# Third token tile from the transposed copy of x, with its statistics stored in front of two broadcasts, and tiles 4 and 5 split in front of tile 3's features

## The chip, the cores and the metric

One core of a Trainium2 chip runs the whole computation as one launch. The metric is the device time of one execution, in microseconds (us). The runs of the kernel before took 638.29, 639.42 and 639.43 us; their median is 639.42 us. All arithmetic is float32; matrix products are made of three passes over operands that are split in a rounded high part and a low remainder.

## What is computed

For x of 2048 tokens by 640 features:

```
xn = layernorm(x)
q, k, v = split(xn @ wqkv)                      # 32 heads of 20
phi(u) = [softmax(u @ w_phi), softmax(-(u @ w_phi))]   # per head
kv = sum over tokens of phi(k)^T v ;  z = sum over tokens of phi(k)
s = (phi(q) kv / (phi(q) z + 1e-6)) @ wo
g = silu(gelu(xn @ w1 + b1) @ w2 + b2)
out = x + s * g
```

The change lies in the first tenth of the execution, where the first six token tiles are normalized, their keys and values are projected, and their key features are made.

## The kernel before

Tokens come in 16 tiles of 128. The matrix unit (TensorE, PE) multiplies token tiles by the folded key weight (`wk_s`, five chunks of 128 rows) and by the value weight (`wv_s`). For that, each tile's normalized x must stand transposed in SBUF (features on partitions, tokens along the row) and split in a high and a low part (`xp`, and `b12` for two chunks of an odd tile). There are two ways to get it:

- **By TensorE.** A tile is loaded as it stands (`x_in`), its mean and variance are taken on VectorE (DVE) (`norm_a`: two bn_stats, one bn_aggr, one add, and a power of -0.5 on GpSimd (POOL)), it is normalized (`norm_b` on DVE, `norm_act` on ScalarE (ACT)), and `transpose_x` turns it by five TensorE transposes into PSUM. `plain` then writes the high part (ACT, L272) and the low part (DVE, L274, reading PSUM). Before, tiles 0, 1 and 2 go this way.
- **From the transposed copy.** The transposed x is loaded from `xt_in` (`one_load` for a single tile, `load_xr` for a pair). Mean and rstd must then lie along the row: they are stored to a small DRAM buffer (`st_dram`) and read back with a partition broadcast as `bc`. POOL subtracts the mean (`one_sub` L370, `pair_sub` L331), DVE multiplies by rstd (`one_plain` L374, `pair_mul` L336), and `plain` splits as above, but now its DVE part reads two SBUF tensors. Before, tile 3 goes this way alone, and tiles 4 and on in pairs.

Per tile t the key path is: `project(t, wk_s)` (30 matmuls of 128x320 into one of three PSUM buffers "A"), `feat1` (DVE: maximum L409, subtraction L412, both reading PSUM, minimum L415; then POOL L416 makes the negated half), `feat2` (ACT exponential L425), `key_fin` (DVE sums L433 and reciprocal L465, then POOL scales, L438). `value(t)` is a projection with `wv_s` and an ACT copy (L454). `kv_pair` accumulates two tiles.

Each engine runs its own instructions in the order of the program, which in this part is mostly the order of the calls in the code; the order in front of the loop over tiles 2 to 5, and in that loop, is written out by hand. SP issues nearly all DMAs, in its own order, and each DMA also waits for the one eight before it. In the loop, tile 3's turn makes its features, then `pair_plain(2)` splits tiles 4 and 5; tile 4's turn holds `pair_sub(3)` and `pair_mul(3)` for tiles 6 and 7, and then `fold_pair(0)`: twelve folding matmuls into two PSUM buffers, then four DVE operations (L188) on them, of which the third is the last to read the first buffer. `value(5)` needs that buffer.

Of the kernel before, what the change touches and what calls it, by code (L numbers as in the profile page):

```python
# [46 lines left out]
def hedgehog_gated_mlp_kernel(ctx: ExitStack, tc: tile.TileContext, x, xt_in, wqk, bd, wv, wo, w1, b1, w2, b2, out_t):  # L47
# [36 lines left out]
    def row(shape, dt, name):  # L84
        return rows.tile(shape, dt, tag="R", name=name)
# [144 lines left out]
    def norm_a(t):  # L230
        sm = small.tile([P, 16], F32, tag="st", name="st")
        nrm[t] = sm, stats(t, sm, None, sm[:, 14:15])
# [6 lines left out]
    def norm_act(t):  # L239
        sm, xt = nrm.pop(t)  # L240
        nc.vector.tensor_scalar(sm[:, 15:16], sm[:, 12:13], -1.0, sm[:, 14:15], op0=OP.mult, op1=OP.mult)
        nc.scalar.activation(xt[:], xt[:], AF.Identity, bias=sm[:, 15:16], scale=sm[:, 14:15])
        xns[t] = xt
# [4 lines left out]
    def load_xr(q):  # L248
        h, p = divmod(q, SLOTS)
        xr = slab(F32, "xr", (P, KC, W2))[:]  # L250
        src = xt_in.rearrange("(k p) (h o q t) -> p k h o q t", p=P, h=NH, o=2, q=SLOTS)[:, :, h, :, p]
        nc.sync.dma_start(xr[:, :, :P], src[:, :, 0])
        nc.sync.dma_start(xr[:, :, P:], src[:, :, 1])
        xrs[q] = xr
# [13 lines left out]
    def plain(q, o, v, only=slice(0, 2), hi=True, lo=None):  # L268
        parts = [(xp[:, 0:5, :, at(q)], v)] if o == 0 else [(beside(q), v[:, 0:2]), (xp[:, 5:8, :, at(q)], v[:, 2:5])]
        parts = parts[only]  # L270
        for dst, src in parts if hi else ():
            nc.scalar.activation(dst[:, :, 0, :], src, AF.Copy)  # L272
        for dst, src in parts if lo is None else ():
            nc.vector.tensor_tensor(dst[:, :, 1, :], src, dst[:, :, 0, :].bitcast(F32), op=OP.subtract)  # L274
        for dst, src in parts if lo else ():
            nc.gpsimd.tensor_tensor(dst[:, :, 1, :], src, dst[:, :, 0, :].bitcast(F32), op=OP.subtract)
# [61 lines left out]
    def pair_plain(q):  # L338
        for o in range(2):
            plain(q, o, xrs[q][:, :, o * P:(o + 1) * P])  # L340

    def one_load(t):
        q = t // 2
        h, p = divmod(q, SLOTS)
        xr = slab(F32, "xr", (P, KC, W2))[:]
        src = xt_in.rearrange("(k p) (h o q t) -> p k h o q t", p=P, h=NH, o=2, q=SLOTS)[:, :, h, t % 2, p]
        nc.sync.dma_start(xr[:, :, :P], src)
        xrs[t, "one"] = xr[:, :, :P]

    def one_stats(t):  # L350
        sm = small.tile([P, 16], F32, tag="st", name="st")
        ps = sm[:, 14:16]
        xt, st = xts.pop(t), sm[:, :12]
        for i in range(2):
            nc.vector.bn_stats(st[:, 6 * i:6 * i + 6], xt[:, i * HALF:(i + 1) * HALF])
        yield
        nc.vector.bn_aggr(sm[:, 12:14], st.rearrange("p (a b) -> p a b", a=2))
        nc.vector.tensor_scalar(ps[:, 1:2], sm[:, 13:14], LN_EPS, None, op0=OP.add)
        nc.gpsimd.tensor_tensor(ps[:, 1:2], ps[:, 1:2], mhalf[:], op=OP.pow)
        nc.vector.tensor_copy(ps[:, 0:1], sm[:, 12:13])  # L360
        nc.sync.dma_start(st_dram[t // 2, t % 2], ps)
        bc = row([P, P, 2], F32, "bc")
        nc.sync.dma_start(bc[:].rearrange("p t s -> p (t s)"),
                          st_dram[t // 2, t % 2].rearrange("p s -> (p s)").partition_broadcast(P))
        pld[t, "one"] = bc
        yield

    def one_sub(t):
        bc, xr = pld[t, "one"], xrs[t, "one"]
        nc.gpsimd.tensor_tensor(xr, xr, bc[:, None, :, 0].to_broadcast([P, KC, P]), op=OP.subtract)  # L370

    def one_plain(t):
        bc, xr = pld.pop((t, "one")), xrs.pop((t, "one"))
        nc.vector.tensor_tensor(xr, xr, bc[:, None, :, 1].to_broadcast([P, KC, P]), op=OP.mult)  # L374
        plain(t // 2, t % 2, xr)

    def transpose_x(t):
        q, o = divmod(t, 2)
        xn = xns.pop(t)
        ps = bankA()  # L380
        flat = ps[:].rearrange("p a b -> p (a b)")
        for k in range(KC):
            nc.tensor.transpose(flat[:, k * P:(k + 1) * P], xn[:, k * P:(k + 1) * P], ident[:])  # L383
        plain(q, o, flat[:, :D].rearrange("p (k t) -> p k t", t=P))
# [3 lines left out]
    def project(t, ws, mid=None, at_k=3):  # L388
        q, o = divmod(t, 2)
        ps = bankA()  # L390
        n = 0
        for k in range(KC):
            if k == at_k and mid is not None:
                mid()
            for a, b in PASSES:
                for hf in range(2):
                    nc.tensor.matmul(ps[:, hf, :HALF], stat_x(q, o, k, a),  # L397
                                     ws[k][:, b, hf * HALF:(hf + 1) * HALF],
                                     start=n == 0, stop=n == 3 * KC - 1)
                n += 1  # L400
        return ps
# [4 lines left out]
    def feat1(ps, later=None):  # L406
        p4 = heads(ps)
        mx = small.tile([P, 2, 16], F32, tag="mx", name="mx")
        nc.vector.tensor_reduce(mx[:], p4, axis=AX.X, op=OP.max)  # L409
        e = slab(F32, "e")[:]  # L410
        e5 = e.rearrange("p a (h s d) -> p a h s d", s=2, d=DH)
        nc.vector.tensor_tensor(e5[:, :, :, 0, :], p4, mx[:, :, :, None].to_broadcast([P, 2, 16, DH]),  # L412
                                op=OP.subtract)
        nr = small.tile([P, 2, 16], F32, tag="nr", name="nr")
        last_feat[0] = nc.vector.tensor_reduce(nr[:], e5[:, :, :, 0, :], axis=AX.X, op=OP.min)  # L415
        rest = lambda: nc.gpsimd.tensor_tensor(e5[:, :, :, 1, :], nr[:, :, :, None].to_broadcast([P, 2, 16, DH]),  # L416
                                               e5[:, :, :, 0, :], op=OP.subtract)
        if later is None:
            rest()
        else:  # L420
            later.append(rest)
        return e.rearrange("p a b -> p (a b)")

    def feat2(ef):
        nc.scalar.activation(ef, ef, AF.Exp)  # L425
        return ef
# [24 lines left out]
    def value(t, mid=None):  # L451
        ps = project(t, wv_s, mid)
        v, v3 = value_row()
        nc.scalar.activation(v3[:, :, :DH].rearrange("p (a h) d -> p a h d", a=2), heads(ps), AF.Copy)  # L454
        return v
# [12 lines left out]
    def key_fin(ef):  # L468
        scale_heads(ef, key_sums(ef))
        return ef  # L470
# [12 lines left out]
    def kv_pair(t):  # L483
        for u in (t, t + 1):
            kv_acc(u, phis.pop(u), vs.pop(u))
# [47 lines left out]
    def x_in(t, eng=None):  # L533
        xts[t] = load_x(t, eng)
# [13 lines left out]
    wv_raw = [load_raw(wv[c * P:(c + 1) * P, :]) for c in range(KC)]  # L548
    for t in (3, 4, 5):
        x_in(t)  # L550
    x_in(6)
    x_in(7)
    nc.sync.dma_start(b1t[:], b1)
    nc.sync.dma_start(b2t[:], b2)
    wv_s = []

    def split_v(c):
        wv_s.append(split_w(wv_raw[c][:], "wv", "dve" if c == 3 else "pool"))
# [10 lines left out]
    norm_a(1)  # L569
    fold_w(wkT, range(4, KC), "wk", wk_s)  # L570
    norm_act(1)
    norm_a(2)
    st3 = one_stats(3)
    next(st3)
    split_v(0)
    one_load(3)
    kvp[0] = bankB("kv")
    pk = project(0, wk_s, lambda: transpose_x(1), 4)
    split_v(1)
    next(st3)  # L580
    load_xr(2)
    norm_act(2)
    split_v(2)
    es[0] = feat1(pk)
    split_v(3)
    pk = project(1, wk_s, lambda: transpose_x(2))
    split_v(4)
    feat2(es[0])
    es[1] = feat1(pk)
    one_sub(3)  # L590
    pair_stats(4)
    vs[0] = value(0)
    pair_stats(5)
    wqT = load_fold(0, (nc.sync,) * KC)
    x_in(8)
    x_in(9)
# [8 lines left out]
    for t in range(2, 6):  # L605
        pk = project(t, wk_s)
        if t % 2:
            kv_pair(t - 3)
        es[t] = feat1(pk)
        if t == 4:  # L610
            next(vf[0])
        if t == 2:
            pair_sub(2)
            pair_stats(6)
            pair_stats(7)
            pair_mul(2)
        if t == 3:
            pair_plain(2)
        if t > 3:
            pair_stats(t + 4)  # L620
        if t in (3, 4, 5):
            spill(t - 3)
        if t == 5:
            x_in(10)
        if t == 4:
            pair_sub(3)
            pair_mul(3)
        vs[t] = value(t)
        if t >= 4:
            fold_pair(t - 4)  # L630
        if t == 5:
            next(vf[0])
        feat2(es[t])
        if t == 4:
            pair_plain(3)
        phis[t] = key_fin(es.pop(t))
    def q_back(c):
        sl = slab(F32R, "wqb")
        wq_b.append(sl)
        nc.sync.dma_start(sl[:, :, :HALF].bitcast(F32), wq_dram[c])  # L640
# [979 lines left out]
```

## Time and profile before

| | us |
|---|---|
| median of the three timed runs | 639.42 |
| the profiled execution | 637.78 |
| its span, first to last instruction | 636.1 |
| PE busy in the span | 631.3 |
| PE busy from 20 to 80 us | 60.0 of 60 |
| DVE busy from 20 to 80 us | 49.57 of 60 |
| POOL busy from 20 to 80 us | 40.38 of 60 |

PE is busy throughout, so what it does not have to do is time saved, and each wait that it is given is time lost. In the rows of the trace, a row's first number is its start in us from the span's start, the second its length; then follow engine, line, operation, what it writes and reads, and, in square brackets, how long the engine had been idle and what ended that. SPq rows are DMA issues.

### The profile page before, as it was taken

To read this page: it belongs to the slowest core of one execution; us is meant where nothing else is said; L and a number is where in the kernel's file an instruction comes from. 1 tells how busy PE (TensorE), PEld (TensorE's weight loads), DVE (VectorE), ACT (ScalarE), POOL (GpSimd) and SP (SyncE) were. 2 spreads that over 40 slices of the span, in tenths; PEclk is the share of its full clock that TensorE was granted. 3 is DMA by queue.
4 is the path that set the end of the run, shared out by engine and by line. 5 is a ranking of instruction groups with operands and counts; after the bars stand their busy time and mean duration, and the time that the engine had idled before them with its cause. 6 is when DMAs were issued, how large, how long until landed. Compare 5 with 4: busy or idle time off the path is not lost.

```text
span 636.1 us, 11441 instructions
## 1 busy us (share of the span) xinstructions
PE 631.3 (99%) x4324; PEld 550.3 (87%) x4324; DVE 511.1 (80%) x790; ACT 259.7 (41%) x390; POOL 432.5 (68%) x376
## 2 busy tenths in 40 slices
PE   9999999999999999999999999999999999999997
PEld 9999999999999998888888888888888888667676
DVE  5887976789887877878979869758798899887586
ACT  3522422334344347243442534842322335455540
POOL 1877466888978857687878876381735678866363
PEclk9999999999999999999999999999999999999999
DMA  9577287393421488359899699697498598969934
GB/s 347 121 227 230 75 286 223 100 344 134 90 76 42 131 304 284 111 106 349 212 287 315 162 385 350 135 319 258 138 245 168 172 176 271 306 181 310 377 110 152
DMA packets 167168, 136.90 MB, mean 215 GB/s; under 512 B 89864, under 2 KB 130824, under 8 KB 166728
## 3 DMA queue, kind: packets, MB, share of 16 engines
q1 hardware_dynamic: 164376, 124.56, 65.9%
q10 hardware_dynamic: 2736, 11.60, 4.7%
q8 instruction: 34, 0.56, 0.4%
q14 instruction: 22, 0.18, 0.1%
HBM read 87.76 MB, written 48.38 MB: 214 GB/s over the span
## 4 chain that ended last, share of the span: by engine, by line
PE 98%; DMA 1%; DVE 0%; SPq 0%; issue 0%
PE pB L1016 26%; PE pB L987 23%; PE pA L397 22%; PE pB L1218 10%; PE pA L710 7%; PE pB L1144 3%; PE pA L164 2%; PE qV L710 2%; PE kv L477 2%; PE qY L710 1%; DMA folds<-in_wqk_dram 1%; PE pB L1126 0%; PE pA L383 0%; DVE y L1228 0%; PE pB L942 0%; DVE xres L1229 0%
## 5 line engine op out<-in xcount | busy, mean ns | idle before, releaser
L1016 PE MATMUL pB<-hs,w2s 128*128 128x512 f32 x720 | 165.9, 389 | 0.0
L1016 PEld LDWEIGHTS pB<-hs,w2s 128*128 128x128 f32 x720 | 135.0, 188 | 28.8 <-issue 0.8
L987 PE MATMUL pB<-xp,w1s 128*128 128x512 f32 x324 | 81.4, 389 | 0.0
L987 PE MATMUL pB<-xd,w1s 128*128 128x512 f32 x324 | 79.3, 389 | 0.0
L438 POOL TENSOR_TENSOR eq<-eq,rc 128x1280 f32<-128x1280 f32 x16 | 37.9, 2371 | 60.6 <-DVE rc L1078 48.4
L987 PEld LDWEIGHTS pB<-xp,w1s 128*128 128x128 f32 x324 | 60.7, 188 | 12.8 <-ACT x L1003 0.3
L987 PEld LDWEIGHTS pB<-xd,w1s 128*128 128x128 f32 x324 | 60.8, 188 | 12.6
L1025 DVE TENSOR_TENSOR y<-pB,y 128x512 f32<-128x512 f32 x100 | 63.1, 675 | 1.8 <-PE pB L1016 1.8
L992 ACT ACTIVATE pB<-pB,b1t 128x512 f32<-128x512 f32 x48 | 31.8, 662 | 77.3 <-DVE pB L1418 29.5
L397 PE MATMUL pA<-wk,xp 128*128 128x320 f32 x384 | 59.6, 310 | 0.0
L425 ACT ACTIVATE e<-e 128x1280 f32<-128x1280 f32 x32 | 40.7, 1271 | 43.3 <-POOL e L416 42.8
L397 PEld LDWEIGHTS pA<-wk,xp 128*128 128x128 f32 x384 | 56.9, 188 | 0.1
L416 POOL TENSOR_TENSOR e<-nr,e 128x640 f32<-128x640 f32 x32 | 44.8, 1402 | 15.9 <-DVE nr L415 15.5
L438 POOL TENSOR_TENSOR e<-e,rc 128x1280 f32<-128x1280 f32 x16 | 38.4, 2407 | 21.0 <-DVE rc L465 21.0
L1065 POOL TENSOR_TENSOR ez<-eq,zrep 128x1280 f32<-128x1280 f32 x16 | 47.4, 2962 | 2.8 <-DMA eq<-e_dram 2.8
L505 POOL TENSOR_TENSOR w1s<-raw,w1s 128x640 fp32r<-128x640 f32 (+1 forms) x18 | 25.4, 1410 | 18.0 <-ACT w1s L504 17.7
L139 POOL TENSOR_TENSOR w2s<-raw,w2s 128x640 fp32r<-128x640 f32 x23 | 36.1, 1589 | 0.2 <-ACT w2s L137 0.2
L998 DVE TENSOR_TENSOR hs<-pB,hs 128x512 fp32r<-128x512 f32 x48 | 32.0, 683 | 3.8 <-ACT hs L994 3.6
L137 ACT ACTIVATE w2s<-raw 128x640 fp32r<-128x640 f32 x24 | 17.2, 735 | 41.5 <-DVE dn L433 12.1
L409 DVE TENSOR_REDUCE mx<-pA 128x32 f32<-128x640 f32 x32 | 25.9, 809 | 8.9 <-PE pA L397 8.6
L994 ACT ACTIVATE hs<-pB 128x512 fp32r<-128x512 f32 x48 | 28.8, 600 | 2.1
L397 PE MATMUL pA<-wq,xp 128*128 128x320 f32 x192 | 29.6, 309 | 0.0
(220 smaller groups left out, 1281.0 us busy)
## 6 DMA issues: line engine op xcount, KB each, us to landing
raw<-in_w_dram SPq DMA_DIRECT2D x42, 320.0 KB
e_dram<-e ACTq DMA_DIRECT2D x16, 640.0 KB
eq<-e_dram SPq DMA_DIRECT2D x16, 640.0 KB
phi_t<-eq SPq DMA_DIRECT2D x64, 160.0 KB
phT<-phi_t SPq DMA_DIRECT2D x20, 512.0 KB
xt<-in_x_dram SPq DMA_DIRECT2D x16, 320.0 KB
xres<-in_xt_dram SPq DMA_DIRECT2D x20, 256.0 KB
out_dram<-xres SPq DMA_DIRECT2D x19, 256.0 KB
```

The costliest lines, as they stand in the source:

```text
L139: eng.tensor_tensor(sl[:, 1, :], raw, sl[:, 0, :].bitcast(F32), op=OP.subtract)
L397: nc.tensor.matmul(ps[:, hf, :HALF], stat_x(q, o, k, a), ws[k][:, b, hf * HALF:(hf + 1) * HALF], start=n == 0, stop=n == 3 * KC - 1)
L416: rest = lambda: nc.gpsimd.tensor_tensor(e5[:, :, :, 1, :], nr[:, :, :, None].to_broadcast([P, 2, 16, DH]), e5[:, :, :, 0, :], op=OP.subtract)
L425: nc.scalar.activation(ef, ef, AF.Exp)
L438: nc.gpsimd.tensor_tensor(e3, e3, rc[:, :, None].to_broadcast([P, 64, DH]), op=OP.mult)
L710: nc.tensor.matmul(bank[ch], q_x(blk, a, q), p_weight(base, f, w, k)[:, b], start=ch not in seen and n == 0, stop=n == len(mms) - 1, skip_ ...
L987: nc.tensor.matmul(bank[ch][:], tl[:, a, off + wo_:off + wo_ + P], mov(blk, b), start=new and n == 0, stop=n == len(mms) - 1, skip_group_c ...
L998: nc.vector.tensor_tensor(hs[:, 1], ps, hs[:, 0].bitcast(F32), op=OP.subtract)
L1016: nc.tensor.matmul(ps[:], ws[i][:, b, d * P:(d + 1) * P], hs[o][i][:, a, :], start=i == n == 0, stop=(i, n) == (GF - 1, 2), skip_group_che ...
L1025: nc.vector.tensor_tensor(y, ps[:], y, op=OP.add)
L1065: nc.gpsimd.tensor_tensor(zv, ef, zf, op=OP.mult)
L1218: nc.tensor.matmul(ps[:, mv], w, o[:, mv], start=first and n == 0, stop=last and n == len(steps) - 1, skip_group_check=True)
```

## The change

Tile 2 no longer goes through TensorE. Its transposed x is loaded by `one_load(2)` in front of the loads of tiles 6 and 7, its statistics are made by `one_stats(2)`, and it is subtracted (`one_sub(2)`), multiplied (`one_mul(2)`, new, cut out of `one_plain`) and split (`plain(1, 0, ...)`, high part in front of `pair_stats(5)`, low part behind it) like tile 3. `norm_a(2)`, `norm_act(2)` and `transpose_x(2)` go. `one_stats` stops once more between store and broadcast, so that SP stores tile 2's statistics, loads tile 3's transposed x, stores tile 3's statistics, and then issues both broadcasts; b1 and b2 are loaded behind these. In the loop, `pair_plain(2)` stands in front of tile 3's `feat1`, and `pair_sub(3)` moves from tile 4's turn to the end of tile 3's.

```diff
         nc.sync.dma_start(st_dram[t // 2, t % 2], ps)
+        yield
         bc = row([P, P, 2], F32, "bc")
...
-    def one_plain(t):
+    def one_mul(t):
         bc, xr = pld.pop((t, "one")), xrs.pop((t, "one"))
         nc.vector.tensor_tensor(xr, xr, bc[:, None, :, 1].to_broadcast([P, KC, P]), op=OP.mult)
-        plain(t // 2, t % 2, xr)
+        return xr
+
+    def one_plain(t):
+        plain(t // 2, t % 2, one_mul(t))
...
     for t in (3, 4, 5):
         x_in(t)
+    one_load(2)
     x_in(6)
     x_in(7)
-    nc.sync.dma_start(b1t[:], b1)
-    nc.sync.dma_start(b2t[:], b2)
...
     norm_act(1)
-    norm_a(2)
-    st3 = one_stats(3)
+    st2, st3 = one_stats(2), one_stats(3)
+    next(st2)
+    next(st2)
     next(st3)
+    one_load(3)
     split_v(0)
-    one_load(3)
...
     next(st3)
+    next(st2)
+    next(st3)
+    nc.sync.dma_start(b1t[:], b1)
+    nc.sync.dma_start(b2t[:], b2)
     load_xr(2)
-    norm_act(2)
...
-    pk = project(1, wk_s, lambda: transpose_x(2))
+    pk = project(1, wk_s)
     split_v(4)
+    one_sub(2)
     feat2(es[0])
     es[1] = feat1(pk)
+    pair_stats(4)
+    x2 = one_mul(2)
+    vs[0] = value(0)
+    plain(1, 0, x2, lo=False)
+    pair_stats(5)
     one_sub(3)
-    pair_stats(4)
-    vs[0] = value(0)
-    pair_stats(5)
+    plain(1, 0, x2, hi=False)
...
             kv_pair(t - 3)
+        if t == 3:
+            pair_plain(2)
         es[t] = feat1(pk)
...
-        if t == 3:
-            pair_plain(2)
...
         if t == 4:
-            pair_sub(3)
             pair_mul(3)
...
         phis[t] = key_fin(es.pop(t))
+        if t == 3:
+            pair_sub(3)
```

New line numbers are up to 12 higher: L371, L375, L416, L420 and L442 of the changed kernel are L370, L374, L412, L416 and L438 of the one before.

On POOL, between the last split of a value weight and the scaling of tile 0's features, the kernel before has this order; "e<-nr,e" is the negated half of tile 1's features, "xr<-xr,bc" is tile 3's subtraction, "pst" are the powers for tiles 4 and 5, "v" the constant columns of a value tile:

```order
L139 TENSOR_TENSOR wv<-raw,wv 128x640
L416 TENSOR_TENSOR e<-nr,e 128x32x20
L370 TENSOR_TENSOR xr<-xr,bc 128x5x128
L223 TENSOR_TENSOR pst<-pst,mhalf 128x1
L447 MEMSET v 128x32
L448 MEMSET v 128x32
L223 TENSOR_TENSOR pst<-pst,mhalf 128x1
L438 TENSOR_TENSOR e<-e,rc 128x1280
```

The changed kernel has this at the same place:

```order
L139 TENSOR_TENSOR wv<-raw,wv 128x640
L371 TENSOR_TENSOR xr<-xr,bc 128x5x128
L420 TENSOR_TENSOR e<-nr,e 128x32x20
L223 TENSOR_TENSOR pst<-pst,mhalf 128x1
L451 MEMSET v 128x32
L452 MEMSET v 128x32
L223 TENSOR_TENSOR pst<-pst,mhalf 128x1
L371 TENSOR_TENSOR xr<-xr,bc 128x5x128
L442 TENSOR_TENSOR e<-e,rc 128x1280
```

Tile 2's subtraction (the first L371) stands in front of tile 1's negated half, and tile 3's has moved behind both powers.

On DVE, in the turns of tiles 2 and 3, the kernel before has this, from the product for tiles 4 and 5 ("xr<-xr,bc") to tile 3's sums; "rc" are tile 2's sums and reciprocal, "mx", "e" and "nr" tile 3's features, the three L274 the low parts of tile 4 (one row) and tile 5 (two):

```order
L336 TENSOR_TENSOR xr<-xr,bc 128x1280
L433 TENSOR_REDUCE rc<-e 128x64
L465 RECIPROCAL rc<-rc 128x64
L409 TENSOR_REDUCE mx<-pA 128x32
L412 TENSOR_TENSOR e<-pA,mx 128x32x20
L415 TENSOR_REDUCE nr<-e 128x32
L274 TENSOR_TENSOR xp<-xr,xp 128x5x128
L274 TENSOR_TENSOR b_701<-xr,b_701 128x2x128
L274 TENSOR_TENSOR xp<-xr,xp 128x3x128
```

The changed kernel has:

```order
L336 TENSOR_TENSOR xr<-xr,bc 128x1280
L437 TENSOR_REDUCE rc<-e 128x64
L469 RECIPROCAL rc<-rc 128x64
L274 TENSOR_TENSOR xp<-xr,xp 128x5x128
L274 TENSOR_TENSOR b_694<-xr,b_694 128x2x128
L274 TENSOR_TENSOR xp<-xr,xp 128x3x128
L413 TENSOR_REDUCE mx<-pA 128x32
L416 TENSOR_TENSOR e<-pA,mx 128x32x20
L419 TENSOR_REDUCE nr<-e 128x32
```

The three low parts now follow the reciprocal directly, and tile 3's three feature operations follow them.

On POOL, from tile 2's scaling ("e<-e,rc") on, the kernel before has this, with the negated halves of tiles 3 and 4 ("e<-nr,e") and the subtraction for tiles 6 and 7 ("xr<-xr,bc"):

```order
L438 TENSOR_TENSOR e<-e,rc 128x1280
L416 TENSOR_TENSOR e<-nr,e 128x32x20
L447 MEMSET v 128x32
L448 MEMSET v 128x32
L438 TENSOR_TENSOR e<-e,rc 128x1280
L416 TENSOR_TENSOR e<-nr,e 128x32x20
L223 TENSOR_TENSOR pst<-pst,mhalf 128x1
L331 TENSOR_TENSOR xr<-xr,bc 128x5x128 x2
```

The changed kernel has:

```order
L442 TENSOR_TENSOR e<-e,rc 128x1280
L420 TENSOR_TENSOR e<-nr,e 128x32x20
L451 MEMSET v 128x32
L452 MEMSET v 128x32
L442 TENSOR_TENSOR e<-e,rc 128x1280
L331 TENSOR_TENSOR xr<-xr,bc 128x5x128 x2
L420 TENSOR_TENSOR e<-nr,e 128x32x20
L223 TENSOR_TENSOR pst<-pst,mhalf 128x1
```

The subtraction for tiles 6 and 7 now stands in front of tile 4's negated half, so that this half follows it directly.

## The prediction

> **What bounds the kernel now.** I read the page first: engine shares and the chain that ended last. Then the timeline of PE from 0 to 80 us, where the edits lie, and at the same place the timelines of DVE, POOL and SP.
>
> ```profile
> span 636.1 us, 11441 instructions
> PE 631.3 (99%) x4324; PEld 550.3 (87%) x4324; DVE 511.1 (80%) x790; ACT 259.7 (41%) x390; POOL 432.5 (68%) x376
> ```
>
> PE is busy for 631.3 of 636.1 us: there is next to no idle time anywhere that could hide a new wait of PE, or that a better order could win back. So the sum is short: PE work removed, minus PE waits added.
>
> ```profile
> 20.49 0.71 PE L383 MATMUL pA<-ident,xt 128*128 128x128 f32 x5
> 20.95 2.00 PE L397 MATMUL pA<-wk,xp 128*128 128x320 f32 x12
> 22.79 4.56 PE L397 MATMUL pA<-wv,xp 128*128 128x320 f32 x30
> 27.19 1.92 PE L397 MATMUL pA<-wv,b 128*128 128x320 f32 x12
> 31.59 4.56 PE L397 MATMUL pA<-wk,xp 128*128 128x320 f32 x30
> 50.68 4.56 PE L397 MATMUL pA<-wk,xp 128*128 128x320 f32 x30
> 67.97 2.02 PE L397 MATMUL pA<-wv,b 128*128 128x320 f32 x12
> ```
>
> Each row starts where the one ahead ends: PE does not wait here. 31.59 is the key projection of tile 2, 50.68 that of tile 4, 67.97 the value projection of tile 5.
>
> **What is removed.** The five transposes of tile 2 (20.49). They delay the next row by 0.46. The 12 matmuls behind them take 22.79 - 20.95 = 1.84; at the 4.40/30 = 0.147 of the row behind, 12 take 1.76. So 0.46 + 0.08 = 0.54 us of PE goes. ACT's normalization and DVE's PSUM read go too; both engines have room. This gain is certain, and it is 0.08% of the time, below the 0.2% (1.28 us) that a measurement of this kernel can tell from no change.
>
> **What is added: tile 2 must come from POOL and DVE in time.** First, when can its subtraction start?
>
> ```profile
> 16.61 0.55 POOL L223 TENSOR_TENSOR st<-st,mhalf 128x1 f32<-128x1 f32 x1 [1.62 <-DVE st L222]
> 24.25 1.57 POOL L139 TENSOR_TENSOR wv<-raw,wv 128x640 fp32r<-128x640 f32 x1
> 28.80 1.59 POOL L370 TENSOR_TENSOR xr<-xr,bc 128x640 f32<-128x640 f32 x1 [1.12 <-DMA bc<-st_dram]
> ...
> 20.77 0.34 SPq L361 DMA_DIRECT2D st_dram<-st  x1
> 23.94 0.33 SPq L363 DMA_DIRECT2D bc<-st_dram  x1
> 46.36 0.82 SPq L322 DMA_DIRECT2D st_dram<-pst  x1
> 51.64 0.34 SPq L324 DMA_DIRECT2D bc<-st_dram  x1
> ```
>
> Tile 2's power ends at 17.16 as before, so SP stores at 17.2. For tile 3, store to broadcast takes 23.94 - 20.77 = 3.2 with a nearly empty queue, and broadcast to subtraction 28.80 - 23.94 = 4.9; behind loads a store takes 51.64 - 46.36 = 5.3. Tile 2's store stands behind the loads of tiles 6 and 7 and the new load of 320 KB, so I take 4.4 of the 3.2 to 5.3: broadcast at 21.6, subtraction at 26.5. It can't start before 25.8, when the split at 24.25 ends, nor do I expect it behind 27.4. I call it T = 26.5 (25.8 to 27.4). The stores in front of both broadcasts, and b1 and b2 behind them, keep tile 3's own chain where it was (23.94); those two loads are wanted hundreds of us later: nothing. The Trainium skill (DMA: Bandwidth & Descriptors, Anatomy of one DMA) gives a DMA a fixed cost of about 2.0 us; by that T would be POOL's 25.8 and the sum 4.5 us, but these rows show 3.2 and 4.9.
>
> Next, what DVE and POOL do to each other:
>
> ```profile
> 120.97 3.16 POOL L331 TENSOR_TENSOR xr<-xr,bc 128x640 f32<-128x640 f32 x2
> 124.09 1.27 POOL L416 TENSOR_TENSOR e<-nr,e 128x640 f32<-128x640 f32 x1
> 124.16 2.55 DVE L336 TENSOR_TENSOR xr<-xr,bc 128x1280 f32<-128x1280 f32 x1 [2.60 <-POOL xr L331]
> 44.02 1.49 DVE L336 TENSOR_TENSOR xr<-xr,bc 128x1280 f32<-128x1280 f32 x1 [2.43 <-POOL xr L331]
> 49.81 0.89 DVE L274 TENSOR_TENSOR xp<-xr,xp 128x640 fp32r<-128x640 f32 x1
> 50.62 1.50 DVE L274 TENSOR_TENSOR b<-xr,b 128x256 fp32r<-128x256 f32 x1
> 68.53 0.42 DVE L274 TENSOR_TENSOR b<-xr,b 128x256 fp32r<-128x256 f32 x1
> 49.98 1.86 POOL L416 TENSOR_TENSOR e<-nr,e 128x640 f32<-128x640 f32 x1
> 30.36 0.55 POOL L223 TENSOR_TENSOR pst<-pst,mhalf 128x1 f32<-128x1 f32 x1
> 30.43 0.82 DVE L374 TENSOR_TENSOR xr<-xr,bc 128x640 f32<-128x640 f32 x1 [1.53 <-POOL xr L370]
> ```
>
> At 124 a subtraction is followed on POOL by a negated half; the DVE product that the subtraction releases takes 2.55 instead of 1.49 and ends 1.35 behind the half. So of a DVE operation on two SBUF tensors and a POOL operation, the later one does its work, less 0.14, only when the earlier is done. At 49.8 they alternate: DVE's low part is first, POOL's half (1.86 for 1.27) waits for it, and DVE's next low part (1.50 for 0.42) waits for the half. POOL's tiny power (30.36) holds nothing up. The Trainium skill (SBUF — State Buffer, Who interferes with whom) states this as a lock that blocks the other fully; by it each clash would cost 0.14 more, with four below some 0.5 us, but the rows show the overlap.
>
> The change makes this clash at three more places of the stretch: tile 2's subtraction is followed by tile 1's half, the low parts of tiles 4 and 5 meet tile 2's scaling, and the subtraction for tiles 6 and 7 is followed by tile 4's half.
>
> **The sum.**
>
> ```profile
> 27.53 0.88 DVE L220 BATCH_NORM_STATS2 st<-xt 128x6 f32<-128x320 f32 x2
> 28.76 0.14 DVE L225 COPY pst<-st 128x1 f32<-128x1 f32 x1
> 46.95 0.55 DVE L465 RECIPROCAL rc<-rc 128x64 f32<-128x64 f32 x1
> 47.42 0.76 DVE L409 TENSOR_REDUCE mx<-pA 128x32 f32<-128x640 f32 x1
> 52.04 0.55 DVE L274 TENSOR_TENSOR xp<-xr,xp 128x384 fp32r<-128x384 f32 x1
> 62.95 1.49 DVE L336 TENSOR_TENSOR xr<-xr,bc 128x1280 f32<-128x1280 f32 x1 [3.85 <-POOL xr L331]
> 66.86 0.49 DVE L188 TENSOR_TENSOR sr<-sr,pA 128x320 f32<-128x320 f32 x1
> ...
> 26.41 1.28 POOL L416 TENSOR_TENSOR e<-nr,e 128x640 f32<-128x640 f32 x1 [0.59 <-DVE nr L415]
> 47.65 2.37 POOL L438 TENSOR_TENSOR e<-e,rc 128x1280 f32<-128x1280 f32 x1 [1.57 <-DVE rc L465]
> 55.74 2.37 POOL L438 TENSOR_TENSOR e<-e,rc 128x1280 f32<-128x1280 f32 x1 [3.78 <-DVE rc L465]
> 59.82 3.09 POOL L331 TENSOR_TENSOR xr<-xr,bc 128x640 f32<-128x640 f32 x2
> ```
>
> 1. Subtraction 26.5 to 28.1; tile 1's half to 29.35; the blocked product (0.82) ends at 29.35 + 0.82 - 0.14 = 30.0. Tile 5's statistics on DVE (27.53 to 28.90: 1.4) to 31.4, the low part, of the product's size (0.82), to 32.2.
> 2. Tile 2's key projection could start at 31.59 - 0.54 = 31.05 and wants the low part at its fifth matmul, 31.64: PE waits about 0.55. The gain is spent.
> 3. Tile 3's subtraction waits for that low part, ends at 33.65, its product starts at 33.7 instead of 30.43: 3.25 late. What follows hands over between DVE and POOL without slack (POOL waits for DVE's sums, DVE at 44.02 for POOL), so the product for tiles 4 and 5 is at 47.25 and tile 2's reciprocal ends at 47.50 + 3.2 = 50.7.
> 4. Tile 4's low part runs 50.65 to 51.45; PE is back at 50.7 and wants it at 51.3: a wait of 0.2.
> 5. Tile 2's scaling takes over at 51.45 and, at 2.37 - 0.14, ends at 53.7; the blocked 0.42 ends at 54.0, the next 0.55 at 54.5. Only now come tile 3's features: 54.45 instead of 47.42, 7.0 late.
> 6. Half, exponential, sums and reciprocal follow; without the 0.6 that the half lost at 49.98, tile 3's scaling comes 6.4 late, 62.1 to 64.5. The subtraction for tiles 6 and 7 follows at once, to 67.6 (before: 62.91), tile 4's half to 68.85, the blocked product ends at 68.85 + 1.35 = 70.2 instead of 64.44: 5.8 late.
> 7. The folding behind it keeps its distance, so the third L188 ends at 67.35 + 5.8 = 73.1. The value projection of tile 5 waits for that buffer: 73.15 instead of 67.97. **PE is 5.2 us late**, all earlier gains and waits included.
>
> Behind that PE has no idle time to make it up, so the profiled execution goes from 637.78 to 643.0, the median of the runs (1.64 higher than it) from 639.42 to **644.6**. T alone gives 4.5 (at 25.8) to 6.1 (at 27.4), so 643.9 to 645.5 within this case.
>
> **Rivals.** (a) *VectorE keeps the ports through all three low parts of step 5.* Then scaling waits till 52.3, features start at 52.25, the rest is 2.2 less: +3.0, 642.4. Against it: 49.81 to 52.12, where POOL got in between; for it: the waiting operation there was another. (b) *The broadcast is later still*, T about 28, if the store meets the rest of the load queue and loses 6 instead of 4.4: +6.7, 646.1. (c) *The clashes do not recur*, because starts shift by tenths: steps 1, 3, 5 and 6 lose 1.1, 0.25, 2.2 and 1.05 us, +0.6 is left, 640.0. (d) *Not slower.* DVE idles 2.43 in front of 44.02 and 3.85 in front of 62.95, POOL 3.78 in front of 55.74; if these take up the delay and the third L188 ends before 67.4, where the earlier value projection of tile 5 wants its buffer, only the 0.54 is left: 638.9. That is the point from which it decides; against it, each of these idle times is a wait for the other engine in the same chain, and before the change the buffer was free only 0.62 ahead. The change does what it says: the transposes are gone from PE's order.
>
> **Chances.** My case 0.58, (a) 0.15, (b) 0.08, (c) 0.08, (d) 0.11. Slower by over 0.2%: 0.58 + 0.15 + 0.08 and a little of (c): 0.82. Within 0.2%: (d) and most of (c), 0.16. Faster by over 0.2%: 0.02; no idle time of PE is there to be won. The range runs from 640.4, inside (c), to 646.4, past (b); it leaves out (d), half of (c) and the worst of (b), 0.18.
>
> **What would show it.** Right: waits of PE at the key projections of tiles 2 and 4 of some tenths, one of several us at the value projection of tile 5 released by DVE L188; tile 2's product at about 1.8 instead of 0.82, a split of 0.42 at over 2, the product for tiles 6 and 7 at 2.5. Wrong: L188's third row ending near 67 and PE without waits, or no stretched DVE row.

## The result, and the profile after

The changed kernel is slower. Two series of six runs each stand against the kernel before:

| | before, median us | after, median us | ratio (95% interval) |
|---|---|---|---|
| first series | 639.1 (638.3 to 640.1) | 645.11 (643.9 to 647.6) | 1.0099 (1.0077 to 1.0122) |
| second series | 638.28 (637.5 to 639.3) | 647.28 (644.0 to 648.1) | 1.0128 (1.0107 to 1.0148) |
| profiled execution: time, span | 637.78, 636.1 | 644.18, 642.5 | |

With one more single run, the thirteen times of the changed kernel fall into two groups: seven from 643.9 to 645.3 and six from 646.6 to 648.1. The median of a series depends on how many fall into which. All three profiles of this kernel are from the lower group (643.96 to 644.18). What follows explains that group, and the end of the experiments says what is known of the other.

The first lines of the changed kernel's page, against the same two of before:

```profile
span 642.5 us, 11439 instructions
PE 632.5 (98%) x4319; PEld 551.3 (86%) x4319; DVE 514.1 (80%) x791; ACT 259.1 (40%) x389; POOL 436.0 (68%) x377
```

PE's busy time went up by 1.2 us (632.5 against 631.3), although it has five instructions fewer. So the 6.4 us are not all waiting time: PE also did the same work more slowly somewhere. Next the timeline of PE in the stretch of the change (start, length, line, tiles, count, and the wait ahead in brackets):

```profile
51.55 4.08 PE L401 MATMUL pA<-wk,xp 128*128 128x320 f32 x26 [0.33 <-DVE xp L274]
63.27 2.02 PE L401 MATMUL pA<-wk,b 128*128 128x320 f32 x12 [0.57 <-DVE e L416]
72.91 3.47 PE L401 MATMUL pA<-wv,b 128*128 128x320 f32 x12 [3.66 <-ACT xp L272]
76.22 2.80 PE L401 MATMUL pA<-wv,xp 128*128 128x320 f32 x18
```

The value projection of tile 5 (the 12 matmuls from `b`) starts at 72.91 instead of 67.97: 4.94 us late. The two short waits before it (0.33, 0.57) change nothing in the end, because this one would absorb them. The same row also shows the slower work: its 12 matmuls take 3.47 us, and 2.02 in the kernel before. The view of busy time by stretches tells why (the columns are length, busy time of PE, PE's weight loads, VectorE, ScalarE and GpSimd, then the granted clock, DMA share and GB/s):

```profile
72.90:76.40 3.50, 3.49 (x14) 3.50 (x15) 3.46 (x6) 0.66 (x2) 0.00 (x0) 0.53 0.47 187
76.20:79.20 3.00, 3.00 (x23) 3.00 (x23) 2.90 (x6) 0.14 (x1) 2.25 (x1) 1.00 0.03 5
```

Behind the wait the granted clock is 0.53, and then 1.00 again. That stretch costs 3.47 - 2.02 = 1.45 us. Together 4.94 + 1.45 = 6.39, the difference of the spans. (In the two other profiles of this kernel the half clock begins a little later, so that the 12 matmuls take 3.17 and 2.57 us; the whole value projection loses 1.51 us in both.)

The chain that makes the wait, on VectorE and then on GpSimd:

```profile
27.81 1.88 DVE L375 TENSOR_TENSOR xr<-xr,bc 128x640 f32<-128x640 f32 x1 [0.77 <-POOL xr L371]
47.34 1.49 DVE L336 TENSOR_TENSOR xr<-xr,bc 128x1280 f32<-128x1280 f32 x1 [2.47 <-POOL xr L331]
50.26 0.55 DVE L469 RECIPROCAL rc<-rc 128x64 f32<-128x64 f32 x1
51.41 2.58 DVE L274 TENSOR_TENSOR b<-xr,b 128x256 fp32r<-128x256 f32 x1
54.38 0.81 DVE L413 TENSOR_REDUCE mx<-pA 128x32 f32<-128x640 f32 x1
67.30 2.55 DVE L336 TENSOR_TENSOR xr<-xr,bc 128x1280 f32<-128x1280 f32 x1 [1.95 <-POOL xr L331]
72.28 0.49 DVE L188 TENSOR_TENSOR sr<-sr,pA 128x320 f32<-128x320 f32 x1
```

```profile
26.14 1.64 POOL L371 TENSOR_TENSOR xr<-xr,bc 128x640 f32<-128x640 f32 x1 [0.16 <-DMA bc<-st_dram]
27.72 1.28 POOL L420 TENSOR_TENSOR e<-nr,e 128x640 f32<-128x640 f32 x1
50.96 2.75 POOL L442 TENSOR_TENSOR e<-e,rc 128x1280 f32<-128x1280 f32 x1 [1.58 <-DVE rc L469]
64.14 3.12 POOL L331 TENSOR_TENSOR xr<-xr,bc 128x640 f32<-128x640 f32 x2
67.23 1.27 POOL L420 TENSOR_TENSOR e<-nr,e 128x640 f32<-128x640 f32 x1
```

Read the two fences side by side. At 27.7 the half on GpSimd is first, and VectorE's product, 0.82 of work, takes 1.88. At 51 VectorE's 0.42 of `b` takes 2.58 behind the scaling. At 67 the product takes 2.55 instead of 1.49. These are the three places of the prediction. Tile 3's features start at 54.38 instead of 47.42, and the third L188 ends at 72.77 instead of 67.35. The profile names ACT's L272 (72.12 to 72.85) as the releaser of the wait; the third L188 ended 0.08 us before it, so times alone can't tell these two apart. The code can: that L272 splits tile 6, which this projection does not read, while the buffer that it writes is the one whose last reader is the third L188.

### The profile page after: what moved, and what is told of

It reads as the page before. It is cut to its first block, busy times and chain, and to the rows that moved or that the text cites. A ratio compares the mean times of both kernels' runs of the same rounds, so it can differ in the third digit from the quotient of the medians.

```text
span 642.5 us, 11439 instructions
## 1 busy us (share of the span) xinstructions
PE 632.5 (98%) x4319; PEld 551.3 (86%) x4319; DVE 514.1 (80%) x791; ACT 259.1 (40%) x389; POOL 436.0 (68%) x377
## 4 chain that ended last, share of the span: by engine, by line
PE 88%; DMA 3%; POOL 3%; DVE 2%; SPq 1%; issue 1%; ACT 0%; POOLq 0%
PE pB L1028 25%; PE pB L999 23%; PE pA L401 15%; PE pB L1230 10%; PE pA L722 7%; PE pB L1156 3%; PE qV L722 2%; PE kv L481 1%; PE qY L722 1%; PE pA L164 1%; DMA folds<-in_wqk_dram 1%; POOL xr L331 1%; POOL e L442 1%; DMA bc<-st_dram 1%; DMA st_dram<-pst 1%
## 5 line engine op out<-in xcount | busy, mean ns | idle before, releaser
L442 POOL TENSOR_TENSOR eq<-eq,rc 128x1280 f32<-128x1280 f32 x16 | 37.9, 2371 | 60.6 <-DVE rc L1090 43.4
L420 POOL TENSOR_TENSOR e<-nr,e 128x640 f32<-128x640 f32 x32 | 44.0, 1379 | 18.8 <-DVE nr L419 18.4
L442 POOL TENSOR_TENSOR e<-e,rc 128x1280 f32<-128x1280 f32 x16 | 38.8, 2429 | 20.9 <-DVE rc L469 17.5
```

What stands on the lines that cost most here:

```text
L442: nc.gpsimd.tensor_tensor(e3, e3, rc[:, :, None].to_broadcast([P, 64, DH]), op=OP.mult)
```

## The experiments

Each is the changed kernel with an edit, except e5, which is the kernel before with one. All but e8 and e12 were timed in up to twelve runs against the kernel before, whose medians in these series were 638.1 to 638.3.

**e1: both moves in the loop undone.** In the loop body:

```
-        if t == 3:
-            pair_plain(2)
         es[t] = feat1(pk)
...
             pair_mul(2)
+        if t == 3:
+            pair_plain(2)
...
         if t == 4:
+            pair_sub(3)
             pair_mul(3)
...
-        if t == 3:
-            pair_sub(3)
```

> The changed kernel with its two moves in the loop undone: tile 3's features again in front of the split of tiles 4 and 5, and the subtraction for tiles 6 and 7 again in tile 4's turn. Tile 2 still comes from the transposed copy. Theory (blocked elementwise operations add up along one chain): the first half of the delay stays (product for tiles 4 and 5 at 47.3 us instead of 44.0, tile 2's reciprocal 3.3 us late), the scaling and the product for tiles 6 and 7 (62.95 + 3.3 = 66.3) are at 1.5 us instead of 2.5 again, the third L188 ends at 67.35 + 3.3 = 70.7. The loss shows at the key projection of tile 4 (its low part ends at 50.70 + 3.3 = 54.0, wanted at 51.2: PE waits 2.8 us), and the value projection of tile 5 then waits for less than 1 us more. Time 641.8 us, or 643.2 if a wait of 2.8 us is also followed by slow matmuls as the wait of 3.7 us was. Rival 1 (the loop moves make the whole loss): back at 639. Rival 2 (the moves in the loop cost nothing, tile 2's late start alone makes the loss): 645.

Measured 642.16 us (640.7 to 644.8), ratio 1.0064 (1.0043 to 1.0085). Timelines of PE and VectorE:

```profile
53.81 5.60 PE L401 MATMUL pA<-wk,xp 128*128 128x320 f32 x26 [2.56 <-DVE xp L274]
```

```profile
52.88 0.88 DVE L274 TENSOR_TENSOR xp<-xr,xp 128x640 fp32r<-128x640 f32 x1
66.95 1.49 DVE L336 TENSOR_TENSOR xr<-xr,bc 128x1280 f32<-128x1280 f32 x1 [3.68 <-POOL xr L331]
```

The wait is where it was expected, at the key projection of tile 4, and of the expected size (2.56 for 2.8). In the profiled execution the clock fell behind it, too (the rows stand in the last section): 26 matmuls take 5.60 us for the 4.08 of the changed kernel's row. It did not in every run: the mean granted clock is 1.000 in the two shortest (640.7 and 641.3 us) and 0.996 or 0.997 in the other four. The median is between the two times that were expected. Both rivals fall: neither did the loss go, nor did all of it stay. About half of the delay is made by tile 2's own path, and without the two moves it comes out at an earlier place of PE.

**e2: only tile 5's half of the split behind tile 3's features.**

```
-            pair_plain(2)
+            pair_plain(2, (0,))
         es[t] = feat1(pk)
...
+        if t == 3:
+            pair_plain(2, (1,))
```

> The changed kernel with only tile 5's half of the split moved behind tile 3's features; tile 4's half stays in front of them. Theory: VectorE has only one low part (0.8 us) in front of tile 2's scaling, so features of tile 3 start at 51.5 instead of 54.4 us, the following 2.9 us come earlier, of which tile 3's half, stretched again, takes back 0.6: third L188 ends near 70.4 instead of 72.8, PE waits about 2.2 us instead of 3.7 + 0.5 in front of the value projection of tile 5. Time 642.8 us (641.5 if the shorter wait leaves the clock alone). Rival (the delay in tile 3's features is taken up by idle time of VectorE and GpSimd further on): 645, third L188 at 72.8.

Measured 640.42 us (640.1 to 643.5), ratio 1.0038 (1.0023 to 1.0053). PE, then VectorE:

```profile
69.52 1.99 PE L401 MATMUL pA<-wv,b 128*128 128x320 f32 x12 [1.60 <-ACT xp L272]
```

```profile
49.75 0.55 DVE L469 RECIPROCAL rc<-rc 128x64 f32<-128x64 f32 x1
50.90 0.81 DVE L413 TENSOR_REDUCE mx<-pA 128x32 f32<-128x640 f32 x1
68.89 0.49 DVE L188 TENSOR_TENSOR sr<-sr,pA 128x320 f32<-128x320 f32 x1
```

The features start 3.48 us earlier than in the changed kernel (50.90 for 54.38), of which 0.51 stands already at the reciprocal (49.75 for 50.26); the third L188 ends 3.39 earlier (69.38 for 72.77). So 2.97 us are won at 51 and 2.88 of them arrive at 69: no idle time in between takes them up. The forecast of 70.4 was 1.0 too late: half of that is the 0.51, and half is that tile 3's half was less held up (1.39 us) than in the kernel before (1.86). The time is 1.1 us under the lower of the two that were expected. The wait of 1.6 us left the clock alone (1.99). With the clock, this is the largest single part of the loss.

**e3 and e8: matmuls in the wait.** In front of the value projection of tile 5, 24 of them in e3 and 12 in e8:

```
+        if t == 5:
+            pw = bankB("fill")
+            for i in range(24):
+                nc.tensor.matmul(pw[:, :HALF], stat_x(2, 0, i % KC, 0), wv_s[i % KC][:, 0, :HALF],
+                                 start=True, stop=True)
         vs[t] = value(t)
```

> The changed kernel with 24 matmuls more, of the size of a projection's, into a bank that nobody reads, in front of the value projection of tile 5, where TensorE would wait 3.7 us. Theory (TensorE's clock falls because it stood idle): granted clock 1.0 behind the wait, the 12 matmuls in 1.8 to 2.0 us instead of 3.47, time 645.1 - 1.45 = 643.7 us, the value projection still at 72.9. Rival (the 12 matmuls are slow for another reason, what VectorE and the loads do at that time): they keep 3.4 us, and the time is 645.1.

> The changed kernel with 12 instead of 24 unread matmuls in front of the value projection of tile 5, so that TensorE stands still for 1.9 us instead of 3.7. A wait of 1.6 us left the clock alone and one of 2.6 us halved it. Theory (what counts is the length of the standstill): matmuls behind it at 147 ns, clock 1.0. Rival (what counts is the share of idle time over a longer stretch with the first matmuls in it): 267 ns again. Value projection at 72.9 in both.

Measured 643.91 us (643.1 to 646.1) for e3, 643.56 in the one run of e8. PE of e3, then of e8:

```profile
72.68 1.99 PE L401 MATMUL pA<-wv,b 128*128 128x320 f32 x12
```

```profile
72.69 1.99 PE L401 MATMUL pA<-wv,b 128*128 128x320 f32 x12 [1.72 <-ACT xp L272]
```

The start is that of the changed kernel (72.62 to 72.91 in its three profiles), but the 12 matmuls take 1.99 us, beside the same VectorE work and loads. So the slow matmuls come from PE's standstill, and the standstill of 1.72 us in e8 did not bring them. Only about half of the 1.45 us arrives at the end: four of e3's six runs are at 643.1 to 644.2, and the lower group of the changed kernel at 643.9 to 645.3. In e8's profile PE waits 0.5 us behind VectorE's L741 near 156 us, which the changed kernel doesn't: an earlier PE doesn't make the elementwise chain earlier.

**e4: tile 1's half behind tile 2's product.**

```
-    es[1] = feat1(pk)
+    half = []
+    es[1] = feat1(pk, half)
     pair_stats(4)
     x2 = one_mul(2)
+    half[0]()
```

> The changed kernel with GpSimd's negated half for tile 1 put behind tile 2's product in program order, so that nothing is between tile 2's subtraction on GpSimd and its product on VectorE. Theory: the product takes 0.82 instead of 1.88 us (27.8 to 28.6), everything behind it in the chain comes up to 1.06 us earlier, the third L188 ends at 71.7, PE waits 2.7 us instead of 3.7: time 644.0 us (642.6 if the shorter wait leaves the clock alone). Rival (tile 1's half, exponential and sums now come 1 us later and hold up tile 1's scaling and all behind it): no gain, 645 to 646.

Measured 643.62 us (643.0 to 645.2), ratio 1.0086 (1.0070 to 1.0102). PE and VectorE:

```profile
71.61 3.03 PE L401 MATMUL pA<-wv,b 128*128 128x320 f32 x12 [3.66 <-ACT xp L272]
```

```profile
27.60 0.83 DVE L375 TENSOR_TENSOR xr<-xr,bc 128x640 f32<-128x640 f32 x1 [0.63 <-POOL xr L371]
66.00 2.55 DVE L336 TENSOR_TENSOR xr<-xr,bc 128x1280 f32<-128x1280 f32 x1 [1.95 <-POOL xr L331]
```

The product is 0.83 long, and the product for tiles 6 and 7 starts 1.30 earlier than in the changed kernel (66.00 for 67.30), of which 0.21 stands already in the start of tile 2's product (27.60 for 27.81). The value projection is 1.30 earlier, too. Its wait keeps its 3.66 us, not 2.7: with the low parts earlier the two short waits of PE ahead of it are gone, so PE is there earlier as well. A delay of 1.05 us at 28 us was one of 1.1 at 72.

**e5: the kernel before with only the two moves in the loop.**

```
+        if t == 3:
+            pair_plain(2)
         es[t] = feat1(pk)
...
-            pair_sub(3)
             pair_mul(3)
...
+        if t == 3:
+            pair_sub(3)
```

> The kernel before with only the two moves in the loop (split of tiles 4 and 5 in front of tile 3's features, subtraction for tiles 6 and 7 behind tile 3's scaling); tile 2 keeps its five transposes. Theory (the two halves of the delay add): tile 2's reciprocal ends at 47.50 us as in the kernel before, the split and the scaling clash as in the changed kernel, tile 3's features start at 51.1 instead of 47.42, the third L188 ends at 69.5 and the value projection of tile 5 waits 1.5 us at full clock. Time 1.6 us over the kernel before, 639.8 to 640.7. Rival (the moves in the loop alone make the loss of the change): 644 to 645. Rival (the move of the subtraction wins back what the move of the split loses): no difference.

Measured 644.22 us (643.0 to 648.3), ratio 1.0104 (1.0076 to 1.0131), by the total a hit for the first rival. But the profile puts it elsewhere. PE's timeline, then VectorE's:

```profile
70.59 1.99 PE L397 MATMUL pA<-wv,b 128*128 128x320 f32 x12 [1.38 <-ACT xp L272]
244.51 1.60 PE L988 MATMUL pB<-xd,w1s 128*128 128x512 f32 x6 [2.66 <-DVE e L412]
```

```profile
243.54 0.82 DVE L412 TENSOR_TENSOR e<-pA,mx 128x640 f32<-128x640 f32 x1
```

At the value projection of tile 5 the wait is 1.4 us, as expected (1.5). The rest is a wait of 2.66 us at 244, where the next stage begins: its second bank is released by VectorE's last read of query scores. The same two rows in the kernel before, PE and VectorE:

```profile
238.28 1.52 PE L987 MATMUL pB<-xd,w1s 128*128 128x512 f32 x6
```

```profile
240.14 0.83 DVE L412 TENSOR_TENSOR e<-pA,mx 128x640 f32<-128x640 f32 x1
```

There the matmuls start while that read is still to come, so they have another bank. By these rows the new order of the work came with another placing of the banks, which costs e5 some 3 us more than the moves do; how the placing came about isn't shown. So at the value projection of tile 5 the two halves of the delay do add as the theory says, but the total of e5 can't show it. (Its profiled run also started 1.2 us later, at PE's first weights.)

**e6: only the subtraction for tiles 6 and 7 moved back.** The second and the fourth piece of e1's edit.

> The changed kernel with only the subtraction for tiles 6 and 7 moved back to tile 4's turn. By the prediction's step 6 the clash of the product with tile 4's half costs 1.05 us, so without it the third L188 would end at 71.7, time 644.0. Theory now, from the changed kernel's profile: the subtraction then stands behind tile 4's half and a power, starts at 66.0 instead of 64.1 us, the product ends at 70.6 instead of 69.9 though it is short again, the third L188 ends at 73.5, PE waits 0.7 us more: time 645.8. So the move would be worth 0.7 us to the changed kernel and not be a part of the loss.

Measured 647.78 us (644.6 to 648.4), ratio 1.0136 (1.0112 to 1.0159). VectorE, GpSimd and PE:

```profile
69.01 1.49 DVE L336 TENSOR_TENSOR xr<-xr,bc 128x1280 f32<-128x1280 f32 x1 [3.78 <-POOL xr L331]
```

```profile
65.77 3.21 POOL L331 TENSOR_TENSOR xr<-xr,bc 128x640 f32<-128x640 f32 x2
```

```profile
73.56 3.54 PE L401 MATMUL pA<-wv,b 128*128 128x320 f32 x12 [4.43 <-ACT xp L272]
```

The product is short again but ends later, at 70.5 (69.85 in the changed kernel), and the value projection starts 0.65 later. So this move of the change was a gain of 0.65 us (0.9 against the two other profiles of the changed kernel): the clash that it makes (1.06) is less than the wait that it saves. The median is 2.0 above the 645.8 that was expected, and isn't used: four of its six runs are in an upper group, as below. The two others, 644.6 and 644.7 us, are under the 645.8 and inside the lower group of the changed kernel, so the gain shows in the rows and not in the times.

**e7: three places mended.** The edits of e2 and e4, and tile 4's half behind the product for tiles 6 and 7:

```
-        es[t] = feat1(pk)
+        es[t] = feat1(pk, half if t == 4 else None)
...
             pair_mul(3)
+            half.pop()()
```

> The changed kernel with three places mended: tile 1's half behind tile 2's product, tile 5's split behind tile 3's features, and tile 4's half behind the product for tiles 6 and 7. Theory (the blocked operations are the whole loss): tile 2's product and the product for tiles 6 and 7 are at 0.8 and 1.5 us, the third L188 ends at 67.3, the value projection of tile 5 starts at 67.8 without a wait, and what is left is the removed transposes: 0.3 to 0.6 us under the kernel before, 637.8 to 638.8. Rival (tile 2 from the transposed copy costs time of its own, by its loads or its place in the queues): 640 or more, with a wait of PE in the first 100 us.

Measured 638.62 us in twelve runs (637.9 to 640.5), ratio 1.0009 (1.0000 to 1.0018). PE, then VectorE:

```profile
67.69 2.03 PE L401 MATMUL pA<-wv,b 128*128 128x320 f32 x12
157.14 1.14 PE L727 MATMUL pA<-ws,xp 128*128 128x320 f32 x6 [0.47 <-DVE v L741]
```

```profile
63.13 1.49 DVE L336 TENSOR_TENSOR xr<-xr,bc 128x1280 f32<-128x1280 f32 x1 [1.94 <-POOL xr L331]
67.05 0.49 DVE L188 TENSOR_TENSOR sr<-sr,pA 128x320 f32<-128x320 f32 x1
156.60 0.49 DVE L741 TENSOR_TENSOR v<-qu,pA 128x320 f32<-128x320 f32 x1
```

PE has no wait left at tile 5, and the value projection starts 0.28 earlier than in the kernel before. So the three places were the whole loss of the first 75 us. But the gain of the removed transposes doesn't show in the time: PE waits near 157 for VectorE's read of 156.60, and is late from there on. Back from that read, the first row that is late against the kernel before is VectorE's statistics at 93.8, which wait for a load. First e7 (SyncE's queue, then VectorE), then the kernel before (SyncE's queue, VectorE, PE):

```profile
75.86 0.37 SPq L322 DMA_DIRECT2D st_dram<-pst  x1
80.48 0.32 SPq L324 DMA_DIRECT2D bc<-st_dram  x1
87.57 1.44 SPq L132 DMA_DIRECT2D xt<-in_x_dram  x2
```

```profile
93.78 0.89 DVE L220 BATCH_NORM_STATS2 st<-xt 128x6 f32<-128x320 f32 x2 [1.63 <-DMA xt<-in_x_dram]
```

```profile
75.67 0.37 SPq L322 DMA_DIRECT2D st_dram<-pst  x1
78.89 0.32 SPq L324 DMA_DIRECT2D bc<-st_dram  x1
86.06 1.51 SPq L132 DMA_DIRECT2D xt<-in_x_dram  x2
```

```profile
92.82 0.89 DVE L220 BATCH_NORM_STATS2 st<-xt 128x6 f32<-128x320 f32 x2 [0.41 <-DMA xt<-in_x_dram]
155.82 0.49 DVE L724 TENSOR_TENSOR v<-qu,pA 128x320 f32<-128x320 f32 x1
```

```profile
156.50 1.04 PE L710 MATMUL pA<-ws,xp 128*128 128x320 f32 x6
```

From the store of statistics to the broadcast behind it pass 4.62 us instead of 3.22, all that follows in the queue is 1.5 us later, the statistics 0.96, VectorE's read 0.78 and PE 0.64. The rival's signs (640 or more, a wait of PE in the first 100 us) did not come, but its idea may hold in small: a place in the queue, late by 0.2 us at the store, seems to cost what the transposes gave. This chain is read off the rows and no run tests it; between 99.9 and 102.5 us VectorE is back ahead of the kernel before, and from 108.3 us on it is late again. Why the store takes longer to land isn't settled.

**e9 and e12: the changed kernel again; e10 and e11: another place of the later stage.** The edit of e10 in the changed kernel, and of e11 in e7's:

```
         if t == 9:
             next(vb)
-            next(vb)
...
-            for _ in range(4):
+            for _ in range(5):
                 next(vb)
```

> The changed kernel as it is, on the same chip as the next two. Its six runs so far lie between 643.9 and 647.6 us. Theory (VectorE's split at the start of the later stage, near 152 us, runs in one of two ways: 1.2 us, or 3.6 us when GpSimd's scaling goes ahead of it, and TensorE then waits some 2 us more near 156 and 163 us): runs near 644 and runs 2 to 3.5 us above, and a profiled run near 644 shows the 1.2, one near 647 the 3.6. Rival (the spread has nothing to do with that place): a profiled run of 646 or more with the split at 1.2 us.

> The changed kernel with one low part of the later stage (VectorE's first split of a value weight, near 152 us) moved behind the next features, away from GpSimd's subtraction and scaling. Theory: it takes 0.8 us, TensorE does not wait near 156 us, the slow ones of the runs are gone: all of them within about 1 us, median 644.0. The loss of the change in the first 75 us stays as it is (value projection of tile 5 at 72.9, slow matmuls behind it). Rival (the spread comes from elsewhere): still some runs of 646 to 648.

> The kernel with the three places of the changed kernel mended, and the same move of that low part. The three mended places left 638.6 us and a wait of 0.5 us near 156 us behind VectorE's read for the values, with VectorE's work 0.8 us behind that of the kernel before. Theory: the low part is 0.4 us shorter there, the wait falls to about 0.1 us, time 0.4 us lower: 638.2, no difference from the kernel before that can be measured. Rival (the elementwise work that tile 2 now costs GpSimd and VectorE is found missing at another place): 638.6 again, with a wait elsewhere.

> The changed kernel as it is, one more profiled run, for its two groups of times (644.0 to 645.3 and 646.6 to 648.1 us). Theory (VectorE's split near 152 us decides): if the time is 646.5 or more, that row is 3.6 us long and TensorE waits 1 to 2 us near 156 us and 0.8 near 163; if it is 644 to 645.3, the row is 1.2 us and there is no wait. Rival: a time of 646.5 or more with the row at 1.2 us.

Measured: e9 is the second series of the table; e10 646.17 us (644.4 to 647.5); e11 641.04 (639.4 to 641.7); e12 644.08. VectorE near 152 us, in e12, in e3 and in e10:

```profile
151.76 1.20 DVE L660 TENSOR_TENSOR ws<-raw,ws 128x640 fp32r<-128x640 f32 x1
```

```profile
151.11 3.62 DVE L665 TENSOR_TENSOR ws<-raw,ws 128x640 fp32r<-128x640 f32 x1
```

```profile
155.05 4.87 DVE L660 TENSOR_TENSOR ws<-raw,ws 128x640 fp32r<-128x640 f32 x2
```

The profiles of e1, e3 and e6 are from the upper runs of these kernels (644.79, 646.08 and 648.38 us), and all three have the split at 3.62 or 3.63; e3's PE waits 1.71 and 0.84 us behind it. The profiles of the changed kernel, from its lower group, have 1.20 or 1.21 and no such wait. That fits the theory of the two groups, but none of the three profiles of the changed kernel itself fell into its upper group, so for it this stays unproved. A second candidate stands in the runs' granted clocks: the four upper runs of the second series all have a mean of 0.994, its two lower ones 0.997 and 0.999, and 0.994 is also what the profiled executions of e6 and e10 have, where the half clock lasted 6.8 us instead of 3.4. The clock alone doesn't make the group either, since the two upper runs of the first series have 0.996 and 1.000.

e10 was to settle it and does not: its forecast of 644.0 with all runs within 1 us missed. At its new place the moved split stands behind GpSimd's scaling and half, both splits together take 4.87 us, and four of its five runs are at 645.7 us or more. e11 misses its 638.2, too: 641.04, slower than e7. In its profile, of its shortest run (639.43), both splits together take 2.95 us for 2.01 in e7; that this is the cause of the rest is not shown.

## Why the prediction was right, and where it wasn't

Forecast 644.6 us, slower; measured 645.11 in the series that it was made for, and 647.28 in the second, above its range.

- *Removed:* 0.54 us of PE. The value projection of tile 0 is 0.22 earlier in the profiles (22.57 for 22.79), with the start-up row 0.3 later in the profile after.
- *Start of tile 2 (T):* 26.14 us for 26.5, inside 25.8 to 27.4. The broadcast was issued at 21.61, as worked out (21.6), and the subtraction began 4.5 behind it, not 4.9. The 2.0 us that the prediction takes from the Trainium skill (DMA: Bandwidth & Descriptors, Anatomy of one DMA) stands there for DMAs that GpSimd issues; these are issued by SP, and took 4.1 us from the store (17.51) to the broadcast.
- *Steps 1 and 2:* the product is 1.88 long, ends at 29.69 for 30.0. The low part ends at 31.72 for 32.2, and so the wait of PE at tile 2's key projection (0.55) did not come. Nothing depends on it, since the later wait takes in all earlier ones. e4 shows the price of the clash (1.05) alone. The product ends 0.69 behind the half (29.00 + 0.69 = 29.69), so the overlap of 0.14 is there again; by the full lock of the Trainium skill (SBUF — State Buffer, Who interferes with whom) it would be 0.82.
- *Step 3:* the product of tile 3 is at 33.70 for 33.7, though its subtraction (32.09) followed the end of the power ahead of it (32.12) rather than the low part's (31.72). The product for tiles 4 and 5 is at 47.34 for 47.25, the reciprocal to 50.81 for 50.7. That the hand-over between the two engines has no slack is what carried the forecast, and e2 and e4 show it: what is taken off at 51 or 28 us is off at 69 or 72.
- *Steps 4 and 5:* low part to 51.49 for 51.45, a wait of 0.33 for 0.2, features at 54.38 for 54.45.
- *Step 6:* product to 69.85 for 70.2. The clash is there, but e6 shows that the move that makes it is a gain of 0.65 us in sum.
- *Step 7:* 72.91 for 73.15; PE 4.9 us late for 5.2.
- *Failed:* "Behind that PE has no idle time to make it up", taken as the end of the sum. PE's work behind the wait isn't the same work: it costs 1.45 us more at half clock, so the profiled execution is 644.18, not 643.0. The term is missing from the prediction. The step from profile to median (1.64 us, from three runs of the kernel before) filled its place by luck: in later series that median is 638.1 to 638.3, with which the same sum would have given 643.3 to 643.5, under every run of the changed kernel.
- *Not seen either:* the second group of times. The rule that of two clashing operations the one that came first goes first holds at the three places of the change and not at 152 us (below).

The rivals: (a), VectorE keeping the ports through the three low parts, did not happen (2.58 for `b`). (b), T near 28, did not. (c), clashes that don't recur, fell with the three stretched rows. (d), idle time that absorbs the delay, fell with e2 and e4.

## What to carry to other kernels

A chain that two engines hand to and fro without slack carries a delay of 1 us whole to a wait 45 us later, so the price of an elementwise operation that is moved is read at the place where another engine next waits for the chain, not at its own place. Putting a GpSimd operation between a producer on GpSimd and its consumer on VectorE makes the consumer wait for both; putting it behind the consumer cost PE nothing here, though the moved operation itself took 1.52 us (e4) and 2.19 us (e7) instead of 1.28. And a wait of the matrix engine may cost more than its length: about 1.5 us or more at half clock behind waits of 2.56, 3.66 and 4.43 us here, and nothing behind one of 2.66.

## What the runs showed of the hardware

TensorE's clock after a standstill. Waits of 1.38 us (e5), 1.60 (e2) and 1.72 (e8) left 12 matmuls at 1.99 us. Waits of 2.56 (e1), 3.66 (the changed kernel, e4, e10) and 4.43 (e6) were followed by a stretch at a granted clock of 0.50, in which matmuls of 320 columns start 267 ns apart instead of 147, and then by full clock. The length of the wait alone does not decide it: e5's wait of 2.66 us at 244 left the clock at 1.00. Nor does it set the price: the half clock lasted 3.4 us in e1, e4 and the changed kernel (1.45 to 1.53 us lost), but 6.8 us in e6 and in e10 (2.6 and 2.4 us lost), although e10's wait was 3.66, too.

The fall isn't tied to the end of the wait. In e1, whose wait ended at 53.81:

```profile
53.80:54.60 0.80, 0.79 (x4) 0.79 (x5) 0.80 (x1) 0.00 (x0) 0.80 (x1) 0.84 0.80 161
54.60:57.60 3.00, 3.00 (x13) 3.00 (x13) 2.41 (x3) 1.27 (x1) 0.41 (x3) 0.50 1.10 305
```

The first 0.8 us ran mostly at full clock, then came 3.4 us at half.

The profiles agree on a grid. Within each of them, the changes of the clock behind these waits lie a whole number of steps of 3.41 us behind its rise at the start of the execution; in the changed kernel the half clock runs from 72.75 to 76.16. In the step just ahead of each fall PE was busy for 0 to 1.2 us (0.00 in the changed kernel, 0.85 in e1, 1.17 in e10). The emptiest steps behind which the clock stayed full, up to the last 10 us of the execution, had 1.51 us (e5, at 240) and 1.71 us (e3, at 154). In e6 and e10 PE was busy for only part of the first step at half clock (2.34 and 2.00 us), and a second one followed. So it seems to be the work in a step that counts, and with it where a wait lies on the grid, which would also explain why e1's runs differ. This is read off the profiles; no run tests it.

Who goes first of two blocked operations. At 152 us VectorE's split waits for GpSimd's subtraction, and GpSimd's scaling comes right behind that. In the changed kernel (VectorE 0.47 us ahead of the scaling's start) the split goes first and takes 1.21; in e3 (0.58 ahead) the scaling goes first and the split takes 3.62. So having waited longer does not decide it. If runs of one kernel went either way, that would give the two groups of times; it was not seen in two profiles of one kernel.
